# Strassen's scheme in more token blocks of a fused attention and Mish feed-forward kernel, with other edge moves, scales and paired global queries

## The chip, the cores and the metric

The kernel runs on one core of a Trainium2 chip. The metric is the time of one execution on the device in microseconds (us), the median over several executions. Matrix products run on TensorE (PE; the loading of its stationary operand is shown apart as PEld), elementwise work on VectorE (DVE) and ScalarE (ACT), a few reductions over partitions on GpSimd (POOL); transfers are issued by SyncE (SP).

## The reference, cut

```
k_all = concat([k_g, k_l]); v_all = concat([v_g, v_l])        # 8 batches, 8 heads, 512 + 32 tokens, 64 wide
out_g = softmax(scale * q_g @ k_all.T) @ v_all                # 32 global queries see all keys
s_l = concat([scale * q_l @ k_g.T, where(|i - j| <= 32, scale * q_l @ k_l.T, -1e9)])
out_l = softmax(s_l) @ concat([v_g, v_l])                     # local queries: a window and the 32 global keys
x = concat([out_g, out_l])                                    # as 4352 tokens x 512
h = x @ w_in                                                  # 512 -> 2048
g = h * tanh(log1p(exp(h)))
return g @ w_out                                              # 2048 -> 512
```

All operands are float32. The kernel splits an operand into two float16 parts, hi and lo, and makes a product of three TensorE products: hi*hi, hi*lo and lo*hi.

## The kernel before, in words

**Attention.** Two heads share the 128 partitions; a batch has 4 such head pairs (`hp`), each with 4 tiles `t` of 128 queries: 128 units in all, 16 to a batch. A unit is: scores on PE (`scores`, L747), masked maximum on DVE (`row_max`, L762), exponential on ACT with its sum (`expo`, L771), the split into hi (`p_hi`, ACT or DVE through the helper lines L359 and L361) and lo (`p_lo`, L826, DVE), a transposing DMA (`p_turn`, ph to pt), and the product with the values, 12 matmuls of 64 columns into U (`pv`, L843). After four units the result is normalised and split into x hi and lo (`x_norm`, `x_split`) and transposed by DMA into the tile `xx`. A window takes keys of two neighbouring tiles; seven small DMAs per head pair (`v_move`) lay the values out as `va` and `vc` to fit. The global queries of a head pair have their own chain on 64 partitions (`g_scores`, L877; `g_max`; `g_exp`, L899; `g_norm`, L913; `g_turn`; `g_pv`, L942). The scales of q and k of a batch come from maxima over eight loads of 128 x 544 (`b_norm`, L616, DVE).

**Feed-forward.** x goes through it in 17 blocks of 256 tokens, two to a batch; block 16 holds all global tokens. A block has 8 steps of 256 hidden columns. A step: 24 matmuls of 256 columns into h (`m1_mm`, L985), the activation from h to e (`mish`, L1018, ACT), its hi and lo parts into GG (`g_hi`, L359 or L361; `g_lo`, L1038). The second product takes 12 matmuls of 512 columns per step (`m2_mm`, L1050). In the blocks from `FAST` = 14 on it follows Strassen's scheme for a 2 x 2 product of quarters: 7 products instead of 8, each 24 matmuls of 256 columns per block (`product`, L1146), from sums of e (`g_sum`, L1026 to L1028) and sums of `w_out` made once (`w_sums`, `w_diff`, L1109 to L1131), joined in the output tile `ob` (L1165, L1168). The second product of a step stands behind the first products of later steps in TensorE's order.

**Order.** All work is recorded as tasks with a cost for each engine that could do it; class `Plan` simulates the engines with these costs and fixes each engine's order and, where two engines can do a task, which one. `slot(u)` records the tasks of unit u, with the feed-forward step that `M1S` puts there: one step per unit from step 16 on, 9 units behind its number, so that 119 of the 136 steps stand within the 128 units of attention and the remaining two blocks behind it. The first 16 units share TensorE with the scaling and splitting of the weights (`w_norm`, `w_split`). Matmuls on constants (L1416) fill gaps of TensorE at the start.

Of the kernel before, what the change touches and what calls it, by code (L numbers as in the profile page):

```python
# [25 lines left out]
HP = H // 2  # L26
# [5 lines left out]
KW = 640  # L32
# [3 lines left out]
GSC = 2.0 ** -19  # L36
# [15 lines left out]
class Plan:  # L52
# [102 lines left out]
    def order(self):  # L155
# [7 lines left out]
        free = dict.fromkeys((PE, DVE, ACT, POOL, DMA), 0)  # L163
        queue = {e: [] for e in free}
# [22 lines left out]
        def first(e):  # L187

            best = None
            for pri, n, ns, t in queue[e]:  # L190
                t = max(t, free[e]) + (self.TABLE if e == ACT and self.tasks[n][7] not in (None, self.table) else 0)
                if e == DMA and len(ns) > 2:
                    t = max(t, served - ns[2])
                e0 = self.tasks[n][0][0][0]
                if e0 != e and free[e0] <= t + self.LOYAL:
                    continue
                if best is None or t < best[0]:
                    best = (t, pri, e, n, ns)
# [56 lines left out]
def attn_mish_kernel(ctx: ExitStack, tc: tile.TileContext, qt, kt, mxs, vm, vg, qg, w1, w2, consts_in, out, w64):  # L255
# [9 lines left out]
    mask, ident = consts[:, :224], consts[:, 224:]  # L265
# [11 lines left out]
    FAST = 14  # L277
# [4 lines left out]
    def rings(pool, *table):  # L282
        for tag, bufs, shape, dt in table:
# [15 lines left out]
          ("gmx", 2, [64, 4], F32), ("gs", 2, [64, 4], F32), ("gd", 1, [64, 64], F32), ("gpt", 1, [128, 10, 64], F16),  # L299
          ("vmx", 2, [128, 6], F32), ("p2", 3, [128, 1], F32), ("sv", 3, [128, 4], F32),  # L300
# [3 lines left out]
          ("e", 2, [128, 8, 128], F32), ("ob", 1, [128, 2, DM], F32))  # L304
# [90 lines left out]
    ROWS = [(n + 7 - 4 * FAST) % 8 for n in range(8)]  # L395
# [169 lines left out]
    def b_load(b, what=None):  # L565
        if what == "g":
            pl.add(DMA, dma(160), lambda: load(X["qgraw", b], qg[b]), new=[("qgraw", ("qgraw", b))])
# [4 lines left out]
        for tag, kib, src in (("vgraw", 64, vg), ("qgraw", 160, qg)):  # L572
# [22 lines left out]
    def b_scale(b):  # L595
# [4 lines left out]
        def go():  # L600
# [3 lines left out]
            scales(q, s[:, 0:1], s[:, 1:2])  # L604
# [4 lines left out]
    def b_norm(b):  # L609
# [3 lines left out]
        for i in range(8):  # L613
            k = ("mx", b, i)
            pl.add(DMA, dma(272), lambda i=i, k=k: load(X[k][:, :544], mxs[b, i]), new=[("tr", k)])
            pl.add(DVE, dve(544), lambda i=i, k=k: V.tensor_reduce(  # L616
                out=X[mx][:, i:i + 1], in_=X[k][:, :544], axis=AX.X, op=ALU.max,
                apply_absolute_value=True), r=[k], w=[[mx, i]] if i else (), new=() if i else [("mx8", mx)])
# [33 lines left out]
    def k_load(b, hp):  # L652
        pl.add(DMA, dma(320), lambda: load(X["kr", b, hp], kt[b * HP + hp]), new=[("ld", ("kr", b, hp))])
# [837 lines left out]
```

## Time and profile before

| | |
|---|---|
| median of 3 executions | 925.22 us (923.16 to 926.66) |
| the profiled execution | 922.33 us, of which its span is 920.5 us |
| PE busy | 894.3 us (97%), 8444 matmuls |
| DVE busy | 726.4 us (79%) |
| ACT busy | 612.0 us (66%) |
| POOL busy | 18.0 us (2%) |

A span runs from the first to the last instruction; busy shares are shares of it. In the views, a row of the timeline is a group of equal instructions with the start of the first, the time to the end of the last and the count; the ends of pipelined matmuls overlap, so the pitch of a matmul is read from the starts of two neighbouring rows. The last product of attention falls at 85.2, 187.1, 288.2, 388.5, 488.2, 588.4, 688.1 and 787.1 us for the eight batches; what follows is called the tail.

### The profile page before, as it was taken

The page shows a single profiled execution, that of the slowest core. Times are in us where ns is not written, and L with a number is a line of the kernel's source. Part 1 is how long each engine was busy: PE and PEld are TensorE (multiplying, and loading weights), DVE is VectorE, ACT ScalarE, POOL GpSimd, SP SyncE. Part 2 cuts the span into 40 slices and gives each one's busy share as a digit, 9 for nine tenths or more (in the row PEclk, how much of TensorE's full clock was granted, in tenths as well). Part 3 has the DMA queues.
Part 4 walks back from the last instruction along what each step waited for, and adds up shares of the span by engine and source line. Part 5 has one row for each costly group of instructions (what it writes and reads, how often), then busy time and mean ns, then how long its engine had stood idle before and what let it go on. Part 6 is the DMA issues. An engine that isn't in the chain of part 4 may idle for free.

```text
span 920.5 us, 21758 instructions
## 1 busy us (share of the span) xinstructions
PE 894.3 (97%) x8444; PEld 649.5 (71%) x8444; DVE 726.4 (79%) x1940; ACT 612.0 (66%) x1309; POOL 18.0 (2%) x30
## 2 busy tenths in 40 slices
PE   4989999999999999999999999999999999999998
PEld 2767866666767766766766766776776776788887
DVE  6999988868878779787987788877876757798761
ACT  5899786877777768776787768776776667322110
POOL 3000000000000000000000000000000000000000
PEclk9799999999999999999999999999999999999999
DMA  9987358987665878667767867777855554100000
GB/s 331 316 260 254 97 138 161 193 185 185 151 147 123 185 162 179 125 154 172 165 128 153 169 158 162 134 184 165 185 114 124 95 88 77 31 13 2 23 13 35
DMA packets 221399, 132.03 MB, mean 143 GB/s; under 512 B 174320, under 2 KB 186736, under 8 KB 221296
## 3 DMA queue, kind: packets, MB, share of 16 engines
q1 hardware_dynamic: 221296, 130.65, 61.6%
q8 instruction: 66, 1.08, 0.5%
q14 instruction: 37, 0.30, 0.1%
HBM read 66.76 MB, written 8.91 MB: 82 GB/s over the span
## 4 chain that ended last, share of the span: by engine, by line
PE 76%; DVE 8%; DMA 7%; ACT 6%; issue 2%; SPq 1%; POOL 0%; ACTq 0%; DVEq 0%
PE h L985 31%; PE o L1050 26%; PE o L1146 5%; PE U L843 4%; PE s L747 3%; PE g L877 2%; DMA pt<-ph 2%; ACT P L771 1%; DMA mx<-in_mxs 1%; PE gu L942 1%; DVE GG L1038 1%; DVE GG L361 1%; SPq L348 1%; DVE P L762 1%; ACT e L1018 1%
## 5 line engine op out<-in xcount | busy, mean ns | idle before, releaser
L985 PE MATMUL h<-xx,W 128*128 128x256 f16 x3072 | 361.6, 273 | 0.3 <-DMA xx<-xs 0.2
L985 PEld LDWEIGHTS <-W 128*128 128x128 f16 x3264 | 311.4, 98 | 43.0 <-issue 4.3
L1050 PE MATMUL o<-W,GG 128*128 128x512 f16 x1344 | 314.5, 379 | 0.9 <-ACT ob L359 0.9
L1050 PEld LDWEIGHTS <-GG 128*128 128x128 f16 x1344 | 128.7, 98 | 128.5 <-issue 2.4
L1018 ACT ACTIVATE e<-h,c 128x512 f32<-128x512 f32 x136 | 92.7, 687 | 125.1 <-PE h L985 108.2
L771 ACT ACTIVATE P<-P,nm 128x192 f32<-128x192 f32 (+1 forms) x256 | 117.6, 461 | 57.8 <-DVE nm L762 56.4
L1038 DVE SCALAR_TENSOR_TENSOR GG<-e,c,GG 128x512 f16<-128x512 f32 (+1 forms) x136 | 111.3, 819 | 3.6
L361 DVE TENSOR_SCALAR GG<-e,c 128x512 f16<-128x512 f32 (+1 forms) x130 | 78.4, 604 | 39.5 <-ACT e L1018 35.1
L762 DVE CUSTOM_DVE_ANT_0 P<-s,consts 128x192 f32<-128x192 f32 (+1 forms) x256 | 87.5, 364 | 4.4 <-PE s L747 4.4
L826 DVE SCALAR_TENSOR_TENSOR ph<-P,ph 128x448 f16<-128x448 f32 (+1 forms) x112 | 62.8, 587 | 23.2 <-ACT ph L359 22.1
L843 PEld LDWEIGHTS <-pt 96*128 96x128 f16 (+1 forms) x1536 | 60.0, 98 | 27.6 <-issue 5.4
L1018 ACT ACT_TABLE_LOAD x55 | 70.6, 1283 | 3.6 <-PE h L985 2.6
L843 PE MATMUL U<-va,pt 128*128 128x64 f16 (+1 forms) x768 | 56.0, 193 | 2.6 <-DMA pt<-ph 2.1
L359 ACT ACTIVATE ph<-P 128x384 f16<-128x384 f32 (+1 forms) x111 | 55.2, 535 | 0.8 <-DMA pt<-ph 0.7
L843 PE MATMUL U<-vc,pt 96*128 96x64 f16 x768 | 55.4, 193 | 0.0
L1146 PEld LDWEIGHTS <-GG 128*128 128x128 f16 x504 | 49.2, 98 | 6.8 <-DVE GG L1038 1.1
L771 ACT ACTIVATION_READ_ACCUMULATOR P<-P,nm 128x1 f32 x256 | 48.1, 188 | 0.0
L359 ACT ACTIVATE ob<-o,c 128x512 f32<-128x512 f32 (+1 forms) x40 | 24.6, 615 | 32.2 <-PE o L1146 26.7
L771 ACT ACT_TABLE_LOAD x34 | 43.6, 1283 | 0.6
L616 DVE TENSOR_REDUCE mx<-mx 128x1 f32<-128x544 f32 x48 | 34.3, 714 | 10.2 <-DMA mx<-in_mxs 10.2
L1146 PE MATMUL o<-W,GG 128*128 128x256 f16 x360 | 41.6, 273 | 0.5 <-DVE GG L1038 0.5
L359 ACT ACTIVATE xg<-gu,sv 64x32 f32<-64x32 f32 x64 | 20.0, 313 | 24.0 <-PE gu L942 23.5
(159 smaller groups left out, 1029.5 us busy)
## 6 DMA issues: line engine op xcount, KB each, us to landing
mx<-in_mxs SPq DMA_DIRECT2D x48, 272.0 KB, 3.1
out<-ob SPq DMA_DIRECT2D x34, 256.0 KB, 2.9
vl<-in_vm SPq DMA_DIRECT2D x32, 256.0 KB, 4.3
W<-in_w SPq DMA_DIRECT2D x15, 512.0 KB, 6.9
kr<-in_kt SPq DMA_DIRECT2D x24, 320.0 KB, 4.3
vm<-in_vm SPq DMA_DIRECT2D x28, 256.0 KB, 3.4
qr<-in_qt SPq DMA_DIRECT2D x24, 256.0 KB, 4.6
GG<-in_w SPq DMA_DIRECT2D x11, 512.0 KB, 5.8
```

Source lines behind the costliest of these rows:

```text
L359: A.activation(out=dst, in_=src, func=AF.Copy, scale=c)
L361: V.tensor_scalar(dst, src, c, None, ALU.mult)
L616: pl.add(DVE, dve(544), lambda i=i, k=k: V.tensor_reduce(out=X[mx][:, i:i + 1], in_=X[k][:, :544], axis=AX.X, op=ALU.max, apply_absolute_v ...
L762: pl.add(DVE, 69 + 1.04 * w, lambda: V.tensor_tensor_reduce(out=X[P][:, h, :w], in0=X[s][:, c], in1=mask[:, m0:m0 + w], scale=-SCALE, scal ...
L771: pl.add(ACT, 94 + 0.832 * w + 186, lambda: A.activation(out=X[P][:, h, :w], in_=X[P][:, h, :w], func=AF.Exp, bias=X[nm], scale=-1.0, accu ...
L826: pl.add(DVE, dve(n), lambda: V.scalar_tensor_tensor(p_part(X[ph], t, 1), p_src(X[P], t), PSC, p_part(X[ph], t, 0), ALU.mult, ALU.subtract ...
L843: T.matmul(X[u][:, t, h, :], X[pt][:k, p * 4 + h * 2 + c, :], X[vx][:k, t, vl, h * 64:(h + 1) * 64], start=(n == 0), stop=(n == 5))
L985: T.matmul(X[h][:, f * TB:(f + 1) * TB], wh(i, wl)[:, off:off + 128], X[xx][:, d, x, o:o + TB], start=(n == 0), stop=(n == 11))
L1018: pl.add(ACT, 587, lambda: A.activation(out=X[e][:, 0:4].rearrange("p a n -> p (a n)"), in_=X[h], func=AF.Mish, bias=0.0, scale=X[c][:, 0: ...
L1038: pl.add(DVE, dve(n, 1), lambda: V.scalar_tensor_tensor(gdst(blk, i, 1), gsrc(blk, i), X[c][:, 2:3], gdst(blk, i, 0), ALU.mult, ALU.subtra ...
L1050: T.matmul(X[o], GG[:, r, c + f * 2 + t, g, :], wh(8 + i, wl)[:, f * 512:(f + 1) * 512], start=(i == 0 and n == 0), stop=(i == NF - 1 and ...
L1146: T.matmul(X[o][:, :256], GG[:, r, col, g, :], factor(kind, i, wl), start=(fresh_ and n == 0), stop=(n == 23), skip_group_check=True)
```

## The change

- `FAST` is 12: blocks 12 to 16 take the Strassen form of the second product. From `FM` = 15 on, blocks 15 and 16 take one for the first product as well: `m1_fast` makes 42 matmuls of 128 columns per step in two parts (18 and 24) into two h tiles; `m1_join` adds the seven products into e (one copy on ACT or DVE, four additions on DVE), and `mish` then works in place. The sums that it needs are made by `w1_sums` (once per step number) and `x_sums` (once per block), and lie in buffers of attention that are free by then (`HOMES`), so these blocks start after attention's end. `M1S` is less dense within attention: step 16 on runs at 1 in 1.35 units, and 95 steps instead of 119 stand within the 128 units. x of batches 2, 3 and 5 waits in unused rows of GG (`XROW`).
- `g_hi` of the Strassen blocks names ACT first.
- `b_norm` takes a sum of absolute values on ACT (Abs with an accumulated sum) where it took a maximum on DVE; 48 instructions in all, eight for each of batches 2 to 7.
- `v_move` issues 4 DMAs where it issued 7 (batch 0 keeps its own form); `vf` serves as one operand of `pv` directly. k is 576 columns wide instead of 640. `p_hi` and `p_lo` of tiles 1 and 2 are written in two pieces, 2 x 192 and 2 x 32 columns.
- The global queries of two head pairs share a PSUM tile, 64 partitions each: `g_max`, `g_exp`, `g_norm` and `g_turn` run once per two head pairs, on 128 partitions.
- Planner: other constants; `first` now takes the task of highest priority among those that can start within 146 to 156 ns of the earliest; another order of the first loads; 134 filler matmuls instead of 72.

```diff
-WIN = [(0, 192, 32), (128, 224, 0), (288, 224, 0), (448, 192, 0)]
-CHK = [(96, 96), (128, 96), (128, 96), (128, 96)]
-GC = 64
+WIN0 = [(0, 192, 32), (128, 224, 0), (288, 224, 0), (448, 192, 0)]
...
+WIN = [(0, 192, 256), (96, 224, 0), (256, 224, 224), (384, 192, 0)]
+EDGE = [64, 128, 96, 128]
+GC = 128
...
+    LOOK_PE = 0
+    LOOK_DVE = 156
+    LOOK_ACT = 146
+    LOOK_DMA = 156
...
-                if best is None or t < best[0]:
-                    best = (t, pri, e, n, ns)
...
+                if low is None or t < low:
+                    low = t
+                seen.append((t, pri, e, n, ns))
+                if t == free[e]:
+                    break
+            return next((x for x in seen if x[0] <= low + look[e]), None)
...
-    FAST = 14
+    FAST = 12
+    FM = 15
...
-            pl.add(DVE, dve(544), lambda i=i, k=k: V.tensor_reduce(
...
+            pl.add(ACT, act(544) + 93, lambda i=i, k=k: A.activation(
+                out=X[k][:, :544], in_=X[k][:, :544], func=AF.Abs, accum_out=X[mx][:, i:i + 1]), w=[k] + ([[mx, i]] if i else []),
...
-        mv(32, lambda: X[va][0:64, 0], lambda: X[vf][0:64, 0], vf, [va, 0], [("va", va)])
-        mv(128, lambda: X[vc][0:64], lambda: X[vf][64:128], vf, [vc, 0], [("vc", vc)])
...
+        mv(48, lambda: X[vb][64:96, 1:4], lambda: X[vf][96:128, 0:3], vf, [vb, 0], [("vb", vb)] if vb not in pl.place else [])
+        mv(48, lambda: X[vb][32:64, 0:3], lambda: X[vf][0:32, 1:4], vf, [vb, 1])
+        for n in range(2):
+            mv(32, lambda n=n: X[vb][96 * n:96 * n + 32, n::2], lambda: glob(2), g, [vb, 2 + n])
...
+    XROW = {b: r for b, r in ((2, 4), (3, 6), (5, 4)) if 2 * b + 2 <= FAST}
...
+        for n in range(2):
+            rows = slice(64 * n, 64 * n + 64)
+            ks, kl, q = ("ks", b, hp + n), ("kl", b, hp + n), ("qgh", b)
...
+            def products(terms, rows=rows):
...
+                    for i, (x, k) in enumerate(terms):
+                        T.matmul(X[g][rows, c0:c0 + w], x, rhs(k), start=(i == 0), stop=(i == len(terms) - 1))
...
+    FIRST = (("a11", "b11"), ("a12", "b21"), ("s2", "t2")), (("a22", "t4"), ("s1", "t1"), ("s3", "t3"), ("s4", "b22"))
+    PART = {"s2": (0, 0), "s3": (0, 1), "s4": (1, 0), "s1": (1, 1), "t1": (0, 0), "t3": (0, 1), "t4": (1, 0), "t2": (1, 1)}
+    HOMES = ["P"] * 4 + ["pt"] * 3 + ["ph"] * 2 + ["vb"] * 2 + ["ld"] * 3 + ["gph", "gP"]
...
+    def w1_sums(i):
+
+        v = [("w1v", i, n) for n in range(2)]
+        for n in range(2):
+            pl.add(DVE, dve(512), lambda n=n: V.tensor_tensor(flat(v[n]), wh(i, 0)[:, n * 512:n * 512 + 512], wh(i, 1)[:, n * 512:n * 512 + 512],
+                                                              ALU.add), r=[[wslot(i), x] for x in ("hi", "lo")], new=[("wt", v[n])])
+        quarters(v, ((3, 1, 3, ALU.add), (1, 0, 1, ALU.subtract), (0, 3, 0, ALU.subtract), (2, 2, 0, ALU.subtract)))
+        split_sums(v, [("w1s", i, n) for n in range(2)], HOMES[2 * i:2 * i + 2])
...
+    def m1_fast(blk, i, half):
+
+        hn, (b, o) = ("h", blk, i, half), blk_x(blk)
...
+        terms = FIRST[half]
+
+        def go():
+            for k, (x, y) in enumerate(terms):
+                n = 0
+                for c in range(2):
+                    for wl, xl in ((0, 0), (0, 1), (1, 0)):
+                        T.matmul(X[hn][:, k * 128:k * 128 + 128], side_a(x, wl, c), side_b(y, xl, c), start=(k == 0 and n == 0),
+                                 stop=(n == 5), skip_group_check=True)
+                        n += 1
+        keys = blk_parts(blk) + [[wslot(i), "hi"], [wslot(i), "lo"]] + [(k, *x, n) for k, x in (("w1s", (i,)), ("xt", (blk,))) for n in range(2)]
+        pl.add(PE, mm(6 * len(terms), 133), go, r=keys, new=[("h", hn)])
...
+    def m1_join(blk, i):
...
+        pl.add([(ACT, act(128) + 62), (DVE, dve(128))], 0, lambda en: copy(en, x(7, 8), col(hx, 0, 1)), r=[hx], w=[[e, 7]], new=[("e", e)])
+        pl.add(DVE, dve(256), lambda: V.tensor_tensor(x(0, 5, 4), col(hx, 1, 2), two(x(7, 8)), ALU.add), r=[hx, [e, 7]], w=[[e, 0], [e, 4]])
+        pl.add(DVE, dve(256), lambda: V.tensor_tensor(x(5, 7), col(hy, 1, 2), two(x(4, 5)), ALU.add), r=[hy, [e, 4]], w=[[e, 5]])
+        pl.add(DVE, dve(256), lambda: V.tensor_tensor(x(2, 4), col(hy, 0, 2), two(x(6, 7)), ALU.add), r=[hy, [e, 5]], w=[[e, 2]])
+        pl.add(DVE, dve(128), lambda: V.tensor_tensor(x(1, 2), col(hy, 3, 1), x(5, 6), ALU.add), r=[hy, [e, 5]], w=[[e, 1]])
...
-        return ROWS[n // 2 % 8], n % 2 * 4
+        return ROWS[n // 2 % 8 if n < 16 else n // 2 % 4], n % 2 * 4
...
+        if blk >= FM:
+            pl.add(ACT, 587, lambda: A.activation(out=X[e][:, 0:4], in_=X[e][:, 0:4], func=AF.Mish, bias=0.0, scale=X[c][:, 0:1]),
+                   r=[[c, 0]], w=[e], table="mish")
...
-        pl.add([(DVE, dve2(n, 1)), (ACT, act(n, 1))], 0, lambda en: scaled(en, gdst(blk, i, 0), gsrc(blk, i), X[c][:, 2:3]), r=[e, [c, 2]],
+        pl.add([(DVE, dve2(n, 1)), (ACT, act(n, 1))][::1 if blk < FAST else -1], 0, lambda en: scaled(en, gdst(blk, i, 0), gsrc(blk, i), X[c][:, 2:3]), r=[e, [c, 2]],
...
-    LEAD0 = 5.759
-    PACE = -0.374
-    TAIL = 9
+    LEAD0 = 1.571
+    PACE = 0.474
+    TAIL = 6
+    MID = 0.346
...
-        at = int(LEAD0 + PACE * s) if s < 2 * NF else s + TAIL
+        at = int(LEAD0 + PACE * s) if s < 2 * NF else int(min(s + TAIL + MID * (s - 2 * NF), M1S[-1] + 1 if M1S[-1] >= len(UNITS) else 1e9))
...
+    SUMS0 = 42
+    SUMS = 7
+    DIFF0 = 8
+    LATE_S = 4677
+    W1S0 = 6
+    LATE_W = 192
...
+        if u - NU - 2 - W1S0 in range(0, 8 * W1S, W1S) and FM < NBLK:
+            pl.late = LATE_W
+            w1_sums((u - NU - 2 - W1S0) // W1S)
...
-            m1_mm(*m, 0)
-        if t == 2:
+            m1_fast(*m, 0) if fm else m1_mm(*m, 0)
+        if t == 2 and hp % 2 == 0:
...
+            m1_fast(*m, 1) if fm else m1_mm(*m, 1)
+            if fm:
+                m1_join(*m)
+            pl.late = LATE_M
             mish(*m)
+            pl.late = 0
...
+            pl.late = LATE_G
             g_hi(*m1)
             g_lo(*m1)
+            pl.late = 0
```

ScalarE in batch 6, between two loads of its function table (P: scores to exponentials, ph: their parts, e: activations, ob: output), before:

```order
L771 ACTIVATE P_79,sums_0_8883<-P_79,nm_0_2_0_9061 128x224
L771 ACTIVATE P_79,sums_0_8883<-P_79,nm_0_2_1_9065 128x224
L771 ACTIVATE P_80,sums_0_8883<-P_80,nm_0_3_0_9067 128x192
L771 ACTIVATE P_80,sums_0_8883<-P_80,nm_0_3_1_9084 128x192
L359 ACTIVATE ph_85<-P_79 128x2x224
L359 ACTIVATE ph_86<-P_80 128x2x192
L1018 ACT_TABLE_LOAD
L1018 ACTIVATE e_0_9149<-h_0_9070,c_7740 128x512
L1018 ACTIVATE e_1_9194<-h_1_9136,c_7740 128x512
```

and now (mx: the loads for the scales):

```order
L805 ACTIVATE P_80,sums_0_8470<-P_80,nm_0_2_0_8589 128x224
L805 ACTIVATE P_80,sums_0_8470<-P_80,nm_0_2_1_8591 128x224
L805 ACTIVATE P_81,sums_0_8470<-P_81,nm_0_3_0_8625 128x192
L805 ACTIVATE P_81,sums_0_8470<-P_81,nm_0_3_1_8642 128x192
L370 ACTIVATE ph_86<-P_80 128x2x192
L370 ACTIVATE ph_86<-P_80 128x2x32
L627 ACTIVATE mx_1_8540,mx_7_8495<-mx_1_8540 128x544
L1176 ACT_TABLE_LOAD
L1176 ACTIVATE e_0_8697<-h_0_8574,c_7085 128x512
L1176 ACTIVATE e_1_8710<-h_1_8629,c_7085 128x512
L370 ACTIVATE ph_87<-P_81 128x2x192
```

An Abs over 544 columns and a 2 x 32 piece have come in between the exponentials and the activation.

VectorE in block 16, one step of it (e: activations, GG: their parts), before:

```order
L1026 TENSOR_TENSOR e_5_12999<-e_5_12999 128x128
L1027 TENSOR_TENSOR e_5_12999<-e_5_12999 128x256
L1028 TENSOR_TENSOR e_5_12999<-e_5_12999 128x128
L361 TENSOR_SCALAR GG<-e_5_12999,c_12108 128x7x128
L1165 TENSOR_TENSOR ob_12787<-ob_12787 128x256
L1038 SCALAR_TENSOR_TENSOR GG<-e_5_12999,c_12108,GG 128x7x128
```

and now two steps:

```order
L1139 TENSOR_TENSOR e_3_13274<-h_3_0_13228,e_3_13274 128x2x128
L1140 TENSOR_TENSOR e_3_13274<-h_3_1_13249,e_3_13274 128x256
L1141 TENSOR_TENSOR e_3_13274<-h_3_1_13249,e_3_13274 128x256
L1142 TENSOR_TENSOR e_3_13274<-h_3_1_13249,e_3_13274 128x128
L1184 TENSOR_TENSOR e_3_13274<-e_3_13274 128x128
L1185 TENSOR_TENSOR e_3_13274<-e_3_13274 128x256
L1186 TENSOR_TENSOR e_3_13274<-e_3_13274 128x128
L1139 TENSOR_TENSOR e_4_13354<-h_4_0_13306,e_4_13354 128x2x128
L1140 TENSOR_TENSOR e_4_13354<-h_4_1_13329,e_4_13354 128x256
L1141 TENSOR_TENSOR e_4_13354<-h_4_1_13329,e_4_13354 128x256
L1142 TENSOR_TENSOR e_4_13354<-h_4_1_13329,e_4_13354 128x128
L1196 SCALAR_TENSOR_TENSOR GG<-e_3_13274,c_12393,GG 128x7x128
```

The hi part (L361) has left this engine, four additions from h (L1139 to L1142) stand ahead of the sums, and the additions of the next step stand ahead of this step's lo part.

## Rows read from the trace of the kernel before

**Rows 1.** The page: span, engines, and the busy tenths of 40 slices.
```profile
span 920.5 us, 21758 instructions
...
PE 894.3 (97%) x8444; PEld 649.5 (71%) x8444; DVE 726.4 (79%) x1940; ACT 612.0 (66%) x1309; POOL 18.0 (2%) x30
...
PE   4989999999999999999999999999999999999998
...
ACT  5899786877777768776787768776776667322110
```

**Rows 2.** Stretches: bounds, width, busy us (instructions) per engine, clock, DMA share, GB/s.
```profile
0.00:85.20 85.20, 67.69 (x652) 51.18 (x653) 73.45 (x215) 67.69 (x170) 8.94 (x16) 0.88 0.92 304
85.20:187.10 101.90, 99.60 (x893) 68.83 (x894) 88.67 (x243) 83.28 (x172) 1.43 (x4) 1.00 0.69 144
588.40:688.10 99.70, 99.70 (x963) 69.75 (x961) 79.98 (x228) 71.88 (x155) 1.55 (x2) 1.00 0.71 161
688.10:787.10 99.00, 99.00 (x951) 69.27 (x949) 65.86 (x179) 65.96 (x138) 0.00 (x0) 1.00 0.53 96
787.10:920.50 133.40, 129.05 (x1155) 111.52 (x1153) 92.73 (x152) 26.41 (x43) 0.00 (x0) 0.99 0.06 19
```

**Rows 3.** TensorE's waits: for what; us in total, times, longest.
```profile
PE s L747 <- DMA kn<-in_kt: 9.7, 1, 9.7
```

**Rows 4.** Timeline of TensorE: start, us, instruction, count; two stretches.
```profile
866.27 2.78 PE L985 MATMUL h<-xx_g,W 128*128 128x256 f16 x24
868.89 2.78 PE L1146 MATMUL o<-W,GG 128*128 128x256 f16 x24
...
447.58 2.75 PE L1050 MATMUL o<-W,GG 128*128 128x512 f16 x12
450.17 0.25 PE L843 MATMUL U<-va,pt 128*128 128x64 f16 x3
```

**Rows 5.** Timeline of TensorE, narrow matmuls.
```profile
43.09 0.86 PE L493 MATMUL w_s<-W 128*128 128x128 bf16 x12
43.80 0.60 PE L795 MATMUL T<-consts,P 128*128 128x128 f32 x4
...
36.44 0.25 PE L843 MATMUL U<-va,pt 128*128 128x64 f16 x3
36.53 0.25 PE L843 MATMUL U<-vc,pt 96*128 96x64 f16 x3
```

**Rows 6.** Forms: line, engine, out<-in, shapes, count | busy us, mean ns | idle before.
```profile
L616 DVE TENSOR_REDUCE mx<-mx 128x1 f32<-128x544 f32 x48 | 34.3, 714 | 10.2 <-DMA mx<-in_mxs 10.2
...
L359 ACT ACTIVATE ph<-P 128x448 f16<-128x448 f32 x55 | 30.9, 562 | 0.0
L359 ACT ACTIVATE ph<-P 128x384 f16<-128x384 f32 x56 | 28.5, 509 | 0.8 <-DMA pt<-ph 0.7
L1038 DVE SCALAR_TENSOR_TENSOR GG<-e,c,GG 128x896 f16<-128x896 f32 x24 | 27.6, 1151 | 1.2
...
L530 DVE SCALAR_TENSOR_TENSOR W<-W,sw 128x1024 f16<-128x1024 f32 x14 | 17.9, 1279 | 2.8 <-ACT W L359 2.7
...
L471 DVE SCALAR_TENSOR_TENSOR W<-W 128x512 int32<-128x512 int32 x15 | 10.3, 687 | 0.3
...
L1027 DVE TENSOR_TENSOR e<-e 128x256 f32<-128x256 f32 x24 | 10.2, 425 | 0.8
...
L1168 DVE SCALAR_TENSOR_TENSOR ob<-o,c,ob 128x256 f32<-128x256 f32 x9 | 4.4, 484 | 16.8 <-PE o L1146 16.8
```

**Rows 7.** Stretches with ScalarE or VectorE nearly full (columns as in Rows 2).
```profile
80.00:100.00 20.00, 18.89 (x184) 14.91 (x185) 19.89 (x55) 19.74 (x47) 0.00 (x0) 1.00 0.63 167
...
800.00:840.00 40.00, 39.77 (x354) 34.25 (x352) 36.80 (x62) 10.13 (x16) 0.00 (x0) 1.00 0.04 15
```

**Rows 8.** Timeline near the end: the last mish and the last matmul that waits.
```profile
895.34 0.69 ACT L1018 ACTIVATE e<-h,c 128x512 f32<-128x512 f32 x1 [4.55 <-PE h L985]
...
900.69 0.50 PE L1146 MATMUL o<-W,GG 128*128 128x256 f16 x3 [0.31 <-DVE GG L1038]
```

More of the change, by code (lines that the diff above doesn't have):

```diff
@@ L392, in wf @@
         return W[:, j + j // 8 + 1, hf * 512:(hf + 1) * 512]
-    ROWS = [(n + 7 - 4 * FAST) % 8 for n in range(8)]
+    ROWS = (0, 3, 2, 1, 4, 5, 6, 7)
     SPOTS = [20 + r for r in ROWS]
@@ L566, in b_load @@
         if what == "g":
-            pl.add(DMA, dma(160), lambda: load(X["qgraw", b], qg[b]), new=[("qgraw", ("qgraw", b))])
+            pl.add(DMA, dma(128), lambda: load(X["qgraw", b], qg[b]), new=[("qgraw", ("qgraw", b))])
             return
@@ L862, in x_split, with x_keys, x_tile @@
         pl.add(DVE, dve(n), lambda: V.tensor_tensor(X[xs][:, 1, q], flat(), X[xs][:, 0, q], ALU.subtract), r=[x], w=[xs])
+    XROW = {b: r for b, r in ((2, 4), (3, 6), (5, 4)) if 2 * b + 2 <= FAST}
+    def x_keys(b, hp, halves=(0, 1)):
+        if b not in XROW:
+            return [[("xx", b), (hp, half)] for half in halves]
+        return [("GG", XROW[b] + hp // 2, hp % 2 * 4 + part * 2 + half) for part in range(2) for half in halves]
+    def x_tile(b):
+        if b not in XROW:
+            return X["xx", b]
+        return GG[:, XROW[b]:XROW[b] + 2].rearrange("p r c l n -> p (r c l n)").rearrange("p (h a q) -> p h a q", h=HP, a=2)
@@ L870, in g_scores @@
     def g_scores(b, hp, part):
-        ks, kl, q, g = ("ks", b, hp), ("kl", b, hp), ("qgh", b), ("g", b, hp, part)
-        def products(out, terms):
-            a = 0 if part else 32
-            for c0, n, rhs in ((a, 256, lambda k: loc(k, 2 * part, 2)), (0, 32, lambda k: k[:, GC:GC + 32]))[:2 - part]:
-                for i, (x, k) in enumerate(terms):
-                    T.matmul(X[g][:out, c0:c0 + n], x, rhs(k), start=(i == 0), stop=(i == len(terms) - 1))
-        if plain_s(b, hp):
-            kn, kp = pair(b, hp, "kn")
-            pl.add(PE, mm(1, 1024) + 150 + (1 - part) * 90, lambda: products(64, [(X["qgraw", b][:, hp, :], X[kn][:, kp])]),
-                   r=[[kn, kp], ("qgraw", b)], new=bank(g), rows=0.6)
-            return
@@ new lines, in x_sums @@
+    def x_sums(blk):
+        b, o = blk_x(blk)
+        v = [("xv", blk, n) for n in range(2)]
+        for n in range(2):
+            part = lambda l, n=n: x_tile(b)[:, 2 * n:2 * n + 2, l, o:o + TB]
+            pl.add(DVE, dve(512), lambda n=n, part=part: V.tensor_tensor(flat(v[n]).rearrange("p (c n) -> p c n", c=2), part(0), part(1), ALU.add),
+                   r=blk_parts(blk), new=[("wt", v[n])])
+        sub = ALU.subtract
+        quarters(v, ((0, 1, 0, sub), (1, 3, 1, sub), (3, 3, 0, sub), (2, 2, 3, sub)))
+        split_sums(v, [("xt", blk, n) for n in range(2)], [("qs", "vf")[blk % 2]] * 2)
```

355 lines of the change are left out of this document (222 added, 133 removed).

## The prediction

> **What bounds the kernel now.** I read the page first: TensorE is busy for 97% of the span, and from the fifth of the 40 slices to the last but one its digit is 9, while ScalarE's digits run between 6 and 8 in attention and fall to 1 in the tail [rows 1]. The stretches by batch say the same more exactly: batch 1 has 99.6 us of TensorE in 101.9, batch 6 has 99.7 in 99.7, batch 7 has 99.0 in 99.0, the tail 129.05 in 133.4. Only batch 0 is different: 67.69 in 85.2, at a mean granted clock of 0.88 of full speed, with VectorE at 73.45 and ScalarE at 67.69 us [rows 2]. Then the list of TensorE's waits: its longest entry is a single 9.7 us at the start, for the first keys [rows 3]. So the time is an early loss in batch 0, and then TensorE's work laid end to end. A change is worth what it takes from that work, less what the other engines cannot keep up with afterwards, and it may change the early loss. A busy matmul engine is not one at its peak, so I price a matmul by its pitch, from the start of a group to the start of the next.
>
> The profiled execution took 922.33 us, 2.9 below the median of 925.22. The terms below are differences; I put them on the median, which is what will be compared. A measurement of this kernel can tell about 0.5% (4.6 us) from no change.
>
> **Second product in blocks 12 and 13.** The plain form is 8 steps of 12 matmuls of 512 columns: 96 per block. Twelve take 450.17 - 447.58 = 2.59 us, 0.216 each. The Strassen form is 7 x 24 = 168 of 256 columns; 24 of that width take 868.89 - 866.27 = 2.62 us, 0.1092 each [rows 4]. Per block 20.7 us becomes 18.35, so two blocks give **-4.8 us**. The sums that it needs lie on VectorE; I come to that below. The sums of w_out are made once as before, only earlier.
>
> **First product in blocks 15 and 16.** A step had 24 matmuls of 256 columns, 2.62 us. Now it has 42 of 128. The nearest rows are 12 of 128 columns, bf16, each with a weight load of its own: 43.80 - 43.09 = 0.71 us, 0.059 each. Even narrower ones show whether the weight load sets a floor: three of 64 columns, each with its own load, stand 0.09 us apart, 0.030 each [rows 5]. So a load does not hold a matmul to more than about that, and half the pitch of 256 columns, 0.0546, is the lower end. I take 0.057: 2.39 us per step, 0.23 less than before, **-3.6 us** over 16 steps. The ends are -5.3 (0.0546) and -2.3 (0.059).
>
> The Trainium skill ("TensorE: Matmul & The Clock Gate", section "Back-to-back issue gap") says against this that in a stream of pairs of weight load and matmul the spacing at 128 columns is about 81 ns, and that the shorter gap of about 56 ns is that of an isolated matmul. The row with 59 ns is such a stream, so the trace agrees with the page's lower figure. By 81 ns a step would take an estimated 3.4 us.
>
> **The early phase.** Batch 0 and batch 1 carry the splitting of the weights. By the new order eight integer steps of 512 columns (0.69 us each) and six splittings of 1024 (four at 1.28 [rows 6], two at about 0.7) leave VectorE's batch 0 for its batch 1: 12 us. Batch 1 also gets three of the eight sets of sums of w_out (about 13 us by the same forms) and loses eight maxima (0.714 each [rows 6]) and half the global queries' chain (about 4): from 88.67 us [rows 2] it goes to some 102. One more step of the first product (24 matmuls, 2.6 us) stands before the end of batch 1. If batch 0 shortens by all 12 us, batch 1 gives some back: VectorE has 87% of that batch now [rows 2] and 99.5% in the fullest 20 us of the trace, where TensorE loses 1.1 [rows 7]; at 96%, in between, batch 1 would take 107, 5 more than now. That nets -7, with the extra step **-9.6**. If batch 0 does not shorten at all, since neither VectorE (86%) nor ScalarE (79%) fills it and its chains and loads set its length [rows 2], only the loss remains: +5 - 2.6 = **+2.4**. I take **-4**, about the middle.
>
> **Batches 4 to 7: ScalarE against a lighter TensorE.** The change moves 24 steps of the feed-forward behind attention, so TensorE's stretches shrink while ScalarE's work does not. Batch 6: TensorE loses four steps of the first product (4 x 2.62) and 48 matmuls of 512 columns (48 x 0.216): 99.7 becomes 78.8. ScalarE has 71.9 us there [rows 2]. It loses three activations (0.69 each [rows 8]), four exponentials of global queries (0.48 with their sum, by the slope that follows) and two casts of weight sums (0.8 together): -4.8. It gains eight Abs: by the slope between 448 and 384 columns, (562 - 509) / 64 = 0.83 ns per column [rows 6], 544 columns and the reading of the sum make about 0.75, so 6.0. It gains the pieces: seven of 448 columns (562) become 384 (509), one is taken over from VectorE, and eight pieces of 64 columns come at 0.24 by the same slope: +2.1. With 0.7 for one hi part of GG it ends near 75.9, **96% of 78.8**. Batch 5 comes out alike (78 of 81.4); batch 4 and batch 7 stay under 90%. Nothing in the trace runs so full for a whole batch, but a stretch of 20 us has ScalarE at 98.7% (19.74) while TensorE is at 18.89 [rows 7]. If 96% can be had, it costs nothing; at a ceiling of 93% it costs 2.7 + 2.5 = 5 us. I take **+3**. The maxima that leave VectorE (48 of them, 34.3 us [rows 6]) buy nothing here, since TensorE did not wait for VectorE in these batches; halving the global queries' chain and dropping three of seven edge moves count as nothing too, for the same reason: the wait list has no entry of weight for them, and `pv` keeps its 12 matmuls. If that cover were gone they would be gains, so a mistake here is on the good side.
>
> **The tail.** Its work grows from 129 to about 200 us. VectorE, with the hi parts (1.15 us each) handed to ScalarE, has per step of blocks 15 and 16: sums 0.29 + 0.425 + 0.29, the lo part 1.15, the additions of the join 3 x 0.48 + 0.3 (priced by the nearest row that reads PSUM, 484 ns for 256 columns [rows 6]), and 0.23 for the output: about 4.1 us, against 42 x 0.057 + 21 x 0.1092 = 4.69 of TensorE, 88%. The stretch from 800 to 840 us has VectorE at 92% (36.80) and TensorE loses 0.23 of 40 [rows 7], so a mean of 88% is affordable. In the blocks before, the sums of w_in (eight times some 4.4 us) and of x fill what 2 us of slack per step leave. Two places remain. At the very end the chain from the last first product to the last matmuls is now 895.34 to 900.69, of which TensorE waits 0.31 [rows 8]; the join (about 1.9 us) is put in front of the activation, and two products of 2.62 us cover 5.2 of then 6.7: +1.2. And in the one step of each block without a product behind it, a part can find its h tile not yet emptied. I take **+3** in all, between +1 (the end alone) and +8 (half a microsecond in each of 16 steps).
>
> **Sum.** -4.8 - 3.6 - 4 + 3 + 3 = -6.4: 925.2 - 6.4 = **918.8 us**, about 916 for an execution like the profiled one.
>
> **The rivals.**
> 1. *ScalarE paces batches 4 to 6, and the kernel gets slower.* The Abs sums, the pieces and the unchanged 16 table loads per batch meet a TensorE with a fifth less to do. It decides from a ceiling of 89% down: at 87% batch 5 takes 89.8, batch 6 87.2 and batch 4 a little over its own, +18 instead of +3, which gives 934; at 89%, +13 and 929. For it: full batches now have ScalarE at 72% to 82% [rows 2], and the order is fixed beforehand, so a late ScalarE makes TensorE wait at once. Against it: 19.74 of 20 us [rows 7].
> 2. *The early phase gives all it can.* -9.6 instead of -4, and ScalarE's 96% cost nothing: 910. For it: VectorE is what batch 0 loses most work of. Against it: that stretch has no full engine [rows 2].
> 3. *The narrow first product waits for its weight loads, and is slower.* The page has 649.5 us for 8444 loads [rows 1], 0.077 each; if a stream of narrow matmuls cannot run faster than that, 42 make 3.23 us per step, +9.8 instead of -3.6: 932. The pitches of 59 and 30 ns, with a load for each matmul, speak against it [rows 5]. The figure of 81 ns that the Trainium skill states ("TensorE: Matmul & The Clock Gate", "Back-to-back issue gap") would make it an estimated 935; the pitches of [rows 5] do not bear it out.
> 4. *The join eats the gain of blocks 15 and 16.* VectorE takes its instructions in order, and the additions that free the h tiles stand behind lo parts of 1.15 us: +8 instead of +3, 924; the first product's Strassen scheme would then do nothing.
>
> **How the numbers follow.** Forecast (913.5 to 923): 0.48, of which three quarters lie below 920.6, the bound of faster. Rival 1: 0.16, more than half above 929.8. Rival 2: 0.22. Rival 3: 0.04. Rival 4: 0.10, all within 0.5%. Faster: 0.36 + 0.22 = 0.58; slower: 0.09 + 0.04 = 0.13; the same: 0.29. The range takes rival 2 with the narrow matmul at its lower end (908.5) and rival 1 down to a ceiling of 88% (931).
>
> **What would show it.** In the profile of the changed kernel: 42 narrow matmuls in 2.3 to 2.5 us, from the timeline of block 15 or 16; the tail at about 200 us with TensorE over 97% busy; batches 5 and 6 near 81 and 79 us, with ScalarE at 95% and TensorE's waits there under 2 us each. The step of batch 0 is right if its last attention product falls between 74 and 82 us and batch 1 ends between 178 and 187. The prediction is wrong if the list of TensorE's waits has entries of over 10 us for ScalarE's exponentials or parts (rival 1), if the pitch of 128 columns is over 65 ns (rival 3), or if waits for the join or for GG sum to over 5 us (rival 4).

## The result

The changed kernel takes **929.54 us** (928.26 to 930.87), the kernel before 922.95 us in the same comparison: a ratio of 1.0067, 95% interval 1.005 to 1.0083. It is slower by 6.6 us, where 6.4 us less was forecast. The range held the time; the sign was wrong.

The page of the changed kernel, for [rows 1]:

```profile
span 928.5 us, 22806 instructions
...
PE 896.9 (97%) x8918; PEld 666.3 (72%) x8918; DVE 732.0 (79%) x2015; ACT 666.2 (72%) x1442; POOL 18.1 (2%) x34
...
PE   5699999999999999999999999999999999999998
...
ACT  4789888778877777777879988988886454434441
```

TensorE is as full as before. Its stretches, for [rows 2] (bounds, width, busy us and instructions of PE, PEld, DVE, ACT, POOL, clock, DMA share, GB/s):

```profile
0.00:84.00 84.00, 62.54 (x649) 48.24 (x649) 65.14 (x195) 60.42 (x155) 10.08 (x19) 0.94 0.85 281
84.00:192.90 108.90, 107.89 (x961) 75.16 (x961) 102.19 (x264) 87.45 (x188) 3.16 (x5) 1.00 0.67 144
...
480.20:565.10 84.90, 83.46 (x831) 57.23 (x830) 61.79 (x187) 76.09 (x169) 0.97 (x2) 1.00 0.77 166
565.10:646.70 81.60, 81.26 (x818) 56.13 (x820) 60.71 (x193) 70.48 (x164) 0.98 (x2) 1.00 0.77 168
...
722.50:928.50 206.00, 199.87 (x2140) 179.74 (x2137) 163.64 (x357) 88.17 (x129) 0.00 (x0) 1.00 0.05 18
```

The forecast can be laid beside these by its own terms. By the order of the two programs, 396 matmuls of 256 columns and 180 of 512 leave batches 2 to 7 (82.1 us at the pitches of [rows 4]) for the tail. The -4 of the early phase holds 2.6 us for a step that is taken out of later batches, so the end of batch 1 was forecast 1.4 us earlier than before; the 3 us for ScalarE are added to batches 2 to 7, and the tail is what is then left of the forecast span.

| part of the span, us | before | forecast | after | miss |
|---|---|---|---|---|
| to the end of batch 1 | 187.1 | 185.7 | 192.9 | +7.2 |
| batches 2 to 7 | 600.0 | 520.9 | 529.6 | +8.7 |
| tail | 133.4 | 207.5 | 206.0 | -1.5 |

Batch 6 shows what happens in the middle part: TensorE is busy for 81.26 of 81.60 us, so it waits for hardly anything, and the batch is still 2.8 us longer than the 78.8 that its work was priced at. So its work takes longer than priced. The timeline of TensorE there (start, us, instruction, count; first a head pair's tile 0, then its tile 1):

```profile
567.49 0.26 PE L890 MATMUL U<-vf,pt 128*128 128x64 f16 x3 [0.34 <-DMA pt<-ph]
567.69 0.26 PE L890 MATMUL U<-vb,pt 64*128 64x64 f16 x3
567.88 0.26 PE L890 MATMUL U<-vf,pt 128*128 128x64 f16 x3
568.07 0.26 PE L890 MATMUL U<-vb,pt 64*128 64x64 f16 x3
...
574.89 0.25 PE L890 MATMUL U<-vf,pt 128*128 128x64 f16 x3
574.97 0.25 PE L890 MATMUL U<-vb,pt 128*128 128x64 f16 x3
```

Three matmuls of 128 rows take 0.08 to 0.09 us before others of 128 rows, but 0.19 to 0.20 before matmuls of 64 rows, and the way back costs as much. Over the whole trace the last matmul of 64 columns before such a change stands 122 to 126 ns from its successor where 29 is usual: about 95 ns for each change. The new values' layout gives tile 0 an edge operand of 64 rows (`EDGE` begins with 64), where both operands had 96; the paired global queries use 64 columns of weights where 128 were used. That change costs as much:

```profile
568.26 2.79 PE L1050 MATMUL h<-xx,W 128*128 128x256 f16 x24
570.98 0.41 PE L940 MATMUL g<-ks,qgh 128*64 128x256 f16 x2
...
572.07 0.27 PE L940 MATMUL g<-kl,qgh 128*64 128x256 f16 x1
572.27 1.48 PE L1050 MATMUL h<-xx,W 128*128 128x256 f16 x12
```

The 24 matmuls take 2.72 us instead of 2.62, and the last one of 64 columns of weights 0.20 instead of 0.109. Batches 2 to 6 have 16 such changes each before, from the scores of 64 rows, and 36 to 40 after.

The kernel before shows the same price, had I looked for it: its products with the values cost 0.09 us per three when matmuls of 128 rows follow, and 0.18 when the scores do.

```profile
606.77 0.25 PE L843 MATMUL U<-vc,pt 96*128 96x64 f16 x3
606.86 1.47 PE L985 MATMUL h<-xx,W 128*128 128x256 f16 x12
...
631.70 0.25 PE L843 MATMUL U<-vc,pt 96*128 96x64 f16 x3
631.88 0.26 PE L747 MATMUL s<-ks,qs 64*128 64x192 f16 x2
```

The Trainium skill states the rule ("TensorEngine Tiling (Array Packing)", sections "Available Configurations" and "Key Properties"): a change of the tiling mode drains TensorE, and 64 rows or 64 columns are other modes than 128, while 96 stand in no list of modes. It gives no price; the trace agrees and gives about 95 ns.

### The profile page after: what moved, and what is told of

Same layout as the page of the kernel before. It is cut to its first block, busy times and chain, and to the rows that moved or that the text cites. A ratio compares the mean times of both kernels' runs of the same rounds, so it can differ in the third digit from the quotient of the medians.

```text
span 928.5 us, 22806 instructions
## 1 busy us (share of the span) xinstructions
PE 896.9 (97%) x8918; PEld 666.3 (72%) x8918; DVE 732.0 (79%) x2015; ACT 666.2 (72%) x1442; POOL 18.1 (2%) x34
## 4 chain that ended last, share of the span: by engine, by line
PE 69%; DVE 13%; DMA 7%; ACT 7%; issue 2%; SPq 1%; POOL 0%; ACTq 0%; DVEq 0%
PE h L1050 27%; PE o L1208 22%; PE o L1304 7%; PE U L890 5%; PE s L780 3%; DMA pt<-ph 3%; DVE GG L1196 2%; PE g L940 2%; ACT GG L370 2%; SPq L359 1%; PE gu L1007 1%; ACT P L805 1%; DMA wraw<-in_w 1%; PE h L1126 1%; DVE e L1185 1%
## 5 line engine op out<-in xcount | busy, mean ns | idle before, releaser
L1208 PE MATMUL o<-W,GG 128*128 128x512 f16 x1152 | 269.3, 379 | 0.1
L1050 PE MATMUL h<-xx,W 128*128 128x256 f16 x1728 | 200.3, 273 | 0.4 <-ACT e L1176 0.3
L1208 PEld LDWEIGHTS <-GG 128*128 128x128 f16 x1152 | 108.2, 98 | 112.1 <-issue 2.5
L1050 PE MATMUL h<-GG,W 128*128 128x256 f16 x1152 | 136.6, 273 | 0.0
L1196 DVE SCALAR_TENSOR_TENSOR GG<-e,c,GG 128x512 f16<-128x512 f32 (+1 forms) x136 | 117.9, 867 | 13.7 <-ACT GG L370 10.6
L1176 ACT ACTIVATE e<-h,c 128x512 f32<-128x512 f32 x120 | 81.1, 685 | 37.3 <-PE h L1050 32.8
L890 PEld LDWEIGHTS <-pt 128*128 128x128 f16 (+2 forms) x1536 | 63.9, 97 | 32.4 <-issue 8.1
L870 DVE SCALAR_TENSOR_TENSOR ph<-P,ph 128x384 f16<-128x384 f32 x168 | 67.8, 442 | 23.3 <-ACT ph L370 22.0
L370 ACT ACTIVATE GG<-e,c 128x896 f16<-128x896 f32 (+1 forms) x44 | 44.5, 1012 | 47.7 <-DVE e L1186 45.7
L796 DVE CUSTOM_DVE_ANT_0 P<-s,masks 128x192 f32<-128x192 f32 (+1 forms) x224 | 72.2, 369 | 7.4 <-PE s L780 7.2
L372 DVE TENSOR_SCALAR GG<-e,c 128x512 f16<-128x512 f32 x92 | 44.5, 483 | 31.5 <-ACT e L1176 30.9
L890 PE MATMUL U<-vb,pt 128*128 128x64 f16 (+2 forms) x768 | 57.3, 193 | 0.0
L890 PE MATMUL U<-vf,pt 128*128 128x64 f16 x672 | 50.4, 194 | 2.1 <-DMA pt<-ph 2.0
```

What stands on the lines that cost most here:

```text
L370: A.activation(out=dst, in_=src, func=AF.Copy, scale=c)
L372: V.tensor_scalar(dst, src, c, None, ALU.mult)
L796: pl.add(DVE, 69 + 1.04 * w, lambda: V.tensor_tensor_reduce(out=X[P][:, h, :w], in0=X[s][:, c], in1=mask[:, m0:m0 + w], scale=-SCALE, scal ...
L870: V.scalar_tensor_tensor(y, x, PSC, hi, ALU.mult, ALU.subtract)
L890: T.matmul(X[u][:, t, h, :], X[pt][:k, p * 4 + h * 2 + c, :], vx[:k, t, vl, h * 64:(h + 1) * 64], start=(n == 0), stop=(n == 5))
L1050: T.matmul(X[h][:, f * TB:(f + 1) * TB], wh(i, wl)[:, off:off + 128], x_[:, d, x, o:o + TB], start=(n == 0), stop=(n == 11))
```

## The experiments

Each was compared with the kernel before on the same chip; differences between experiments are made from these ratios (1% is 9.2 us). The two runs that change rows alone and the one without fillers keep the order of every engine. Where an instruction moves, to another engine or to a later time, `Plan` fixes another order for all engines, so such a run changes more than its edit names.

**The switch of rows.** One number of the changed kernel:

```diff
-EDGE = [64, 128, 96, 128]
+EDGE = [96, 128, 96, 128]
```

> The changed kernel with one number changed: the edge operand of pv in tile 0 is read with 96 rows instead of 64 (the added rows are zeros). Theory 1 (switches): in the changed kernel 112 times a matmul of 128 rows follows or precedes one of 64 rows within pv, at 123 to 126 ns where 29 is usual; 112 x 0.095 = 10.6 us, so 929.5 - 10.6 = 919. Each attention batch from the second on gets about 1.5 us shorter. Theory 2 (ScalarE paces batches 4 to 6): nothing of ScalarE's is touched, 929 to 930. Theory 3 (the early phase alone lost it): 929 to 930.

Measured: 923.98 us, ratio 1.000 (0.9983 to 1.0016). So some 6 us are these switches, the whole of the loss against the kernel before, and not 10.6. The timeline has lost them; the same place as above, in this kernel:

```profile
561.61 0.26 PE L890 MATMUL U<-vf,pt 128*128 128x64 f16 x3 [0.24 <-DMA pt<-ph]
561.71 0.25 PE L890 MATMUL U<-vb,pt 96*128 96x64 f16 x3
561.80 0.25 PE L890 MATMUL U<-vf,pt 128*128 128x64 f16 x3
561.89 0.25 PE L890 MATMUL U<-vb,pt 96*128 96x64 f16 x3
```

The gain is uneven: batches 2, 3 and 5 are 1.2 to 2.1 us shorter, batch 6 only 0.5 (81.1 instead of 81.6), and the tail is 206.0 us long in both. In batches 3 to 7 TensorE now waits more for the transposed parts. Its waits there (for what: us in total, times, longest; the two largest), first of the changed kernel, then with 96 rows:

```profile
PE U L890 <- DMA pt<-ph: 1.4, 2, 1.1
PE s L780 <- ACT gP L962: 1.0, 1, 1.0
```

```profile
PE U L890 <- DMA pt<-ph: 4.2, 8, 1.6
PE h L1050 <- ACT e L1176: 0.7, 2, 0.4
```

With the smaller ones such waits rise from 2.7 to 5.6 us, which is 2.9 of the some 4 us that do not come back.

The kernel before, with the price added (it leaves out 32 keys):

```diff
-CHK = [(96, 96), (128, 96), (128, 96), (128, 96)]
+CHK = [(96, 64), (128, 96), (128, 96), (128, 96)]
```

> The kernel before, with the second operand of pv in tile 0 read with 64 rows instead of 96 (it leaves out 32 keys of the first tile of each head pair). Same matmuls, same order. Theory 1: 4 switches in each of 32 units, 128 x 0.095 = 12 us: 923 becomes 935. Theories 2 and 3: 923, as before.

Measured: 931.45 us, ratio 1.0084 (1.0053 to 1.0115): 5 to 11 us for 128 switches, again less than the 12 by their pitches. No matmul was added and no other engine's work touched, so neither ScalarE nor the early phase can explain it. Batch 6, 99.7 us in [rows 2], is 101.4 long, again without an idle moment, and 16 x 0.095 = 1.5:

```profile
596.00:697.40 101.40, 101.40 (x963) 70.67 (x961) 80.31 (x228) 72.02 (x155) 1.09 (x2) 1.00 0.69 156
```

**The switch of columns.** With 96 rows, queries beside zeros as weights of 128 columns (called the wide form):

```diff
-("qgh", 1, [128, 2, HP, 64], F16)
+("qgh", 1, [128, 2, 2, 3, 64], F16)
...
-T.matmul(X[g][rows, c0:c0 + w], x, rhs(k), start=(i == 0), stop=(i == len(terms) - 1))
+T.matmul(X[g][:, c0:c0 + w] if wide else X[g][rows, c0:c0 + w], x, rhs(k), start=(i == 0 and not (wide and n)), ...
```

> As the run before, and the global queries' scores of a pair of head pairs are made with 128 columns of weights (64 of queries, 64 of zeros, two accumulated products) instead of two products of 64 columns; same count and order of matmuls. Theory 1 (switches also between 64 and 128 columns, 28 of them at about 0.095): 2.7 us below the run before, 916. If the switch of columns costs nothing: as the run before, 919.

Measured: 925.25 us, ratio 1.0014 (0.9996 to 1.0033), against 1.000 with 96 rows alone: nothing gained. In this form, and in the run on the early phase below, the second product overwrites a part of the first head pair's scores instead of adding to it; the work is the same. In the changed kernel matmuls of 64 columns of weights for the two head pairs start 5 ns apart (at 571.535 and 571.540 us, for one pair), into the two halves of the tile, and that pays for their switches: in batch 6 the first such group and the 24 matmuls ahead of it take 572.27 - 568.26 = 4.01 us by the timeline above, and 567.54 - 563.46 = 4.08 in the wide form, where the 24 alone take 2.62:

```profile
563.46 2.78 PE L1056 MATMUL h<-xx,W 128*128 128x256 f16 x24
566.08 0.38 PE L945 MATMUL g<-ks,qgh 128*128 128x256 f16 x2
...
567.54 1.47 PE L1056 MATMUL h<-xx,W 128*128 128x256 f16 x12
```

**The early phase.** Three runs. The first is on the order of the loads, in the wide form, with 16 constants of the kernel before and its start of the first product; one of the 16 is shown:

```diff
-    ORDER = "w0 k0 m b q0 w8 w1 w4 k3 w11 g w3 w10 w2 w12 q2 k2 w5 k1 w9 w6 w13 q3 w14 q1 w7 w15"
+    ORDER = "m q0 w10 w1 q2 k0 w3 b w0 w5 k1 q1 g k3 w8 w11 k2 w2 q3 w14 w4 w12 w9 w6 w7 w13 w15"
```

> The second run (96 rows, wide global scores) with the order of the first loads, the timing of the weights' conversion and the start of the first product of the kernel before. Theory 3 (in the changed kernel the loads of weights stand behind edge moves in the first 35 us and the converting engines wait for them; batch 1 ended at 192.9 where it ended at 187.1): batch 1 ends 4 to 5 us earlier, 912. If VectorE's work in batches 0 and 1 sets that end whatever the order: 916, no change against the second run.

Measured: 926.37 us, ratio 1.0028 (1.0006 to 1.0051); batch 1 ends at 190.7, one microsecond earlier than in the wide form alone. The loads do arrive earlier: from 20 to 30 us the changed kernel (first) moves 199 GB/s, this run (second) 354.

```profile
20.00:30.00 10.00, 5.90 (x50) 4.02 (x50) 5.91 (x15) 5.67 (x15) 0.00 (x0) 0.89 0.77 199
```

```profile
20.00:30.00 10.00, 6.06 (x48) 3.59 (x44) 9.71 (x26) 8.79 (x23) 0.00 (x0) 0.91 1.06 354
```

VectorE goes from 5.91 to 9.71 us of 10, and the end of batch 1 hardly moves. So the order of the loads is not what lost it. The second run holds the sums of `w_out` back:

```diff
-    r=[[wslot(8 + i), x] for x in ("hi", "lo", "b12")], new=[("wt", v[f])])
+    r=[[wslot(8 + i), x] for x in ("hi", "lo", "b12")] + [("gs", (SUMS0 + SUMS * i - 3) // 16, 0)], new=[("wt", v[f])])
```

> The run with the edge of 96 rows (924.0), with the sums of w_out held back to batches 2 to 5, where they stand in the kernel before; their order alone changes. Theory A (VectorE's work sets the end of batch 1: it was 102 of 108.9 us busy there): batch 1 gets 3 to 5 us shorter and the later batches, where VectorE is at 75%, stay: 919 to 921. Theory B (batch 1 is set by loads and chains): within 1 us of 924. The switches say nothing on it.

Measured: 935.58 us, ratio 1.0136 (1.0113 to 1.0159). Both theories fail on the total, and A on batch 1:

```profile
83.40:191.50 108.10, 105.57 (x950) 73.47 (x951) 91.57 (x235) 87.50 (x186) 3.36 (x6) 1.00 0.69 148
```

VectorE has 91.57 us there instead of 102, and the batch is as long as with 96 rows alone (108.2), so the amount of VectorE's work does not set its length. Batches 3 and 6 became 7 to 8 us longer. The sums stand in batches 2 to 5 in this run, so batch 6 has none of them, and batches 4 and 5, which have some, did not get longer. With the sums the planner moved much else, and which of it cost the 12 us (against 96 rows alone) is not shown.

The third run leaves out the fillers:

```diff
-            for _ in range(self.fill.get(n, 0)):
+            for _ in range(0):
```

> The run with the edge of 96 rows (924.0), without the 134 matmuls on constants; all else in the same order. If the 62 that the change added lie on the path: up to 134 x 0.109 = 14.6 us less in batches 0 and 1, 6.8 of them from the change; if they stand in waits: no change, and if they hold the granted clock up, batches 0 and 1 get longer at a lower clock.

Measured: 928.59 us, ratio 1.0066 (1.0043 to 1.0089). Batch 0 got 2.4 us longer, at a mean granted clock of 0.86 where 0.92 was granted with them, and batch 1 stayed at 108.2. Its stretch, and its longest wait:

```profile
85.90:194.10 108.20, 102.48 (x915) 70.31 (x916) 102.18 (x264) 87.34 (x188) 3.09 (x5) 1.00 0.66 147
```

```profile
PE w_s L504 <- DVE W L482: 3.1, 3, 2.1
```

The fillers stand in waits, and taking them away costs. They are also a part of what looks like a full TensorE: 45 of them (5.7 us) stand in batch 1 of the changed kernel, and 11 (2.7 us) before.

**ScalarE.** With 96 rows, maxima on VectorE for batches 5 to 7 only:

```diff
+            if b >= 5:
+                pl.add(DVE, dve(544), lambda i=i, k=k: V.tensor_reduce(
+                    out=X[mx][:, i:i + 1], in_=X[k][:, :544], axis=AX.X, op=ALU.max,
...
```

> The run with the edge of 96 rows (924.0), with the scales of batches 5 to 7 (worked in batches 4 to 6) from maxima on VectorE again, as in the kernel before. Theory (ScalarE took up the time that the switches gave back: with 96 rows batches 4 to 7 got only 3 us shorter and waits for transposed parts rose): batches 4 to 6 get 1 to 2 us shorter each, 920 to 922. Rival (the waits are those of the transposing DMAs): 924.

Measured: 920.33 us, ratio 0.9972 (0.9955 to 0.9989), against 1.000 with the Abs sums: the one version here that is faster than both kernels, by less than what counts as a difference. The trace is of its slowest execution (924.80 us), and TensorE's waits for transposed parts in batches 3 to 7 are not shorter there (6.7 us, 4.2 with the Abs sums), so it does not show where the gain comes from.

> The changed kernel with its 64 rows, and the maxima of batches 5 to 7 on VectorE. If TensorE's switches cover what ScalarE holds up (TensorE the later of the two): 928 to 929.5, next to nothing. If ScalarE paces on its own: 3 us less, 926.

The same edit with the 64 rows (`EDGE` as in the change): 926.96 us, ratio 1.0051 (1.0031 to 1.007), against 1.0067. And with the wide global scores (there with one start for the bank, so that both products add up):

> 96 rows at the edge, maxima on VectorE for batches 5 to 7 (920.3 so far), and the global queries' scores with 128 columns of weights (queries beside zeros, accumulated). If the 28 switches of columns cost what their pitch shows (0.095 each) and no wait takes it: 917.6. If waits take it, as in the second run: 920.

923.06 us, ratio 1.0008 (0.9995 to 1.002), against 1.0014 for the wide form with the Abs sums. The wide form itself, 3 us slower here than narrow products (0.9972), is again no gain, and both expectations lay too low. Three pairs point the same way, by 0.6 to 2.6 us, and the two intervals of each pair overlap. That ScalarE holds TensorE up a little in batches 4 to 6, as the forecast's +3 said, fits this but is not shown apart from the new order. All of it is far from rival 1's +18.

> 96 rows at the edge, and all 48 scale reductions on VectorE again, those of batches 2 to 4 too, which are worked in batches 1 to 3, where VectorE is at 66% to 94%. If ScalarE is what batches 1 to 3 wait for as well: 917 to 919, below the 920.3 with late maxima alone. If VectorE is (94% in batch 1): 921 to 925.

```diff
-            pl.add(ACT, act(544) + 93, lambda i=i, k=k: A.activation(
...
+            pl.add(DVE, dve(544), lambda i=i, k=k: V.tensor_reduce(
...
```

All 48 maxima on VectorE: 925.58 us, ratio 1.002 (1.000 to 1.0041). Batch 1 is 110.9 us long, 2.7 more than with 96 rows alone, and the whole 4 to 5 us slower than with late maxima only: for batches 2 to 4 the move to ScalarE is right.

**The two Strassen schemes.** With 96 rows, the first product plain:

> The run with the edge of 96 rows (924.0), with Strassen's scheme for the first product undone in blocks 15 and 16: 384 matmuls of 256 columns instead of 672 of 128, no sums of w_in and x, no join. By the pitch of 56 ns in the trace the scheme is worth 16 x (2.62 - 42 x 0.0564) = 4 us less 2 to 3 us of waits: 925 to 926. If VectorE's extra work in the tail (35 us of sums, 1.9 us of join a step) costs more than that: 920 to 923.

```diff
-    FM = 15
+    FM = NBLK
```

Measured: 926.07 us, ratio 1.0036 (1.0019 to 1.0052), so the narrow first product is worth some 3 us. Its own place, the tail, is 207.4 us long here and 206.0 with it: TensorE works 203.45 us instead of 199.86, 3.6 more, and is idle for 3.95 instead of 6.14. The trace is of the slowest execution (930.06 us), so its stretches of attention say nothing on the rest. And the second product of blocks 12 and 13 plain as well:

> 96 rows at the edge, Strassen's scheme only where the kernel before has it (second product of blocks 14 to 16, none in the first product). Against the run with the first product undone (926.1) the second product of blocks 12 and 13 is plain again: +4.2 by the pitches of the trace, 930, if TensorE's work decides in the tail; 926 if VectorE's sums had eaten that gain.

```diff
-    FAST = 12
-    FM = 15
+    FAST = 14
+    FM = NBLK
```

Measured: 931.22 us, ratio 1.0096 (1.0074 to 1.0119): 5 us more. The tail is 213.4 us long, 6.0 more, of which 1.3 are 12 matmuls of the first product that stand there in addition. Both schemes take the work away that they should. No run tests the planner's other constants and choice rule by themselves.

## Why the prediction was wrong, point by point

- **Second product in blocks 12 and 13, -4.8.** Right: plain again, it costs 5 us, and 4.7 by the tail.
- **First product in blocks 15 and 16, -3.6.** Right for TensorE's work: 3.6 us by the tails with and without it, of which 2.2 go into waits. Six matmuls of 128 columns start 0.33 us apart, so 42 take 2.34 us; 2.39 was forecast. From the timeline of block 16:

```profile
885.49 0.83 PE L1126 MATMUL h<-xx_g,W 128*128 128x128 f16 x12
886.16 0.50 PE L1126 MATMUL h<-xt,ph 128*128 128x128 f16 x6
886.49 0.50 PE L1126 MATMUL h<-xt,W 128*128 128x128 f16 x6
886.83 0.50 PE L1126 MATMUL h<-xt,vb 128*128 128x128 f16 x6
887.16 0.50 PE L1126 MATMUL h<-xt,ph 128*128 128x128 f16 x6
887.50 0.50 PE L1126 MATMUL h<-xx_g,vb 128*128 128x128 f16 x6
887.83 0.38 PE L1304 MATMUL o<-W,GG 128*128 128x256 f16 x2
```

  Each has a weight load of its own, so rival 3 falls: 56 ns a matmul is measured. The 81 ns of the Trainium skill ("TensorE: Matmul & The Clock Gate", section "Back-to-back issue gap") do not hold in this trace.
- **Tail, +3.** About right: 206.0 against 207.5, with TensorE idle for 6.1 us where it was for 4.35. Rival 4 did not come: the waits for the join and for GG are 1.4 and 0.6 us.
- **Batches 4 to 7, +3 for ScalarE.** No run contradicts the size, but its working was off: ScalarE was priced at 75.9 us in batch 6 and has 70.48, 86% of the batch instead of 96%; in batch 5 it has 76.09, 90%. In batches 4 to 6 TensorE is idle for 1.8 us in all, so rival 1 did not come either. The first step that failed stands in the same paragraph: "`pv` keeps its 12 matmuls" was taken as a cost of nothing. The count was right, the shapes were not looked at. 112 switches of rows and 28 of columns came with the edge moves and the pairing; the rows alone cost 6 us in time (10.6 by their pitches, of which other waits take up a part when they go). Edits that were costed at nothing "on the good side" held one of the two terms that turned the sign.
- **The early phase, -4.** The second step that failed, by 6 to 7 us. "About the middle" took batch 0 to shorten by some 6 of 12 us; 85.2 became 84.0, although VectorE lost 8 us of work there and ScalarE 7. The end of the bound that spoke of chains was nearer, and the row that said so was there: no engine fills that batch. Batch 1 was to be 5 us longer and is 7.0 longer, 0.7 of it by switches of rows. VectorE's work there came as forecast (102.19 us; the terms listed for it add up to 104, not 102), but it does not set the batch: with 91.57 us of it the batch is as long. TensorE's 107.89 of 108.9 do not set it either, since without fillers it has 102.48 in the same 108.2. A share of busy time was taken for a limit. What does set batches 0 and 1 is open: it is not the order of the loads, the sums or the fillers alone.

Together: the switches, 6 us in time, and the early phase, 6 to 7 us, make the 13 us between forecast and result. The first are shown by runs; the second is read from the stretches, and its cause stays open. Without the switches the kernel is as fast as the one before. By the stretches of the run with 96 rows, against the kernel before with the moved work taken to where it now stands, the tail then gains 6.9 us, the early phase loses 2.0, and batches 2 to 7 lose 6.2, where 3 were forecast; 4.0 of these are more idle time of TensorE. That the time came out inside the range is luck: of the two rivals that bound it, neither happened.

## What to carry to other kernels

Price a matmul by its neighbours too: list the row and column sizes in the order in which they run, and count the changes between 64 and 128. Zero rows that brought an operand from 64 to 96 rows cost nothing here (0.09 us for three matmuls, as with 128) and took the change away. Work moved out of a stretch that no engine fills bought 1.2 us there, for 8 us of VectorE's and 7 of ScalarE's. And before a full engine is called the limit, look at what fills it: fillers count as busy.

## What the runs showed of the hardware that I had not expected

- A change between matmuls of 64 and of 96 or 128 rows, or between weights of 64 and 128 columns, holds TensorE for about 95 ns each way, although its rows say busy (busy for 101.40 of 101.40 us in the kernel before with 64 rows).
- Two products of 64 columns of weights into the two halves of a PSUM tile run side by side (their starts 5 ns apart), which pays for their two changes: 4.01 us against 4.08 in the wide form.
- Stalls inside a full TensorE can hide waits for other engines: of 10.6 us of stalls taken away, 6 came back in time, and 2.9 us of new waits appeared in batches 3 to 7.
